# A planned one-core kernel on Trainium2: one weight step moved from ScalarE to VectorE, row-group products placed whole, column sums placed first

## The chip, the cores and the metric

The kernel runs on one core of a Trainium2 chip. The metric is the device time of one execution in microseconds (us). The engines are TensorE (PE; its weight loads PEld), VectorE (DVE), ScalarE (ACT), GpSimd (POOL) and SyncE (SP), which here only issues DMAs. The profiler gives the granted TensorE clock of each stretch, 1.00 for the upper of its two levels (2.4 GHz) and 0.50 for the lower (1.2 GHz).

## The reference

Three layers on 3072 tokens (4 sequences of 768), with a width of 256. The weight matrices are float64 and arrive as two 32-bit words a number; the kernel turns them into float32 itself.

```python
# 1: gated linear attention, 8 heads of 32, state of 16; cum = running sum of log a
y  = (C B^T * exp(cum_i - cum_j) * causal) x  +  C state * exp(cum)
state = exp(sum(log a)) * state + sum_j (B_j x_j) * exp(cum_last - cum_j)
# 2: gated feed-forward, d_ff = 1536
xn = y / sqrt(mean(y*y) + 1e-6) * rms_g
x  = (silu(xn @ w_gate) * (xn @ w_val)) @ w_out
# 3: channel mix, d_ff = 1024; x_prev is x one token earlier
xk, xr = mu_k*x + (1-mu_k)*x_prev, mu_r*x + (1-mu_r)*x_prev
out = sigmoid(xr @ w_r) * (relu(xk @ w_k)**2 @ w_v)
```

## The kernel before

**Tiles.** The tokens go in 6 tiles of 512 (128 of each sequence). Tile c has an attention stage (scores, masks, state products y), a norm, a first feed-forward stage `ffn1` of 12 units and a second one `ffn2` of 8 units. While `ffn1` of tile t runs, the attention of tile t + 1 is placed between its units (`attend`). For t = 0 there is no `ffn2` yet; `ffn2` of tile t - 1 follows `ffn1` of tile t. Each large product is made of three matmuls of 128 x 128 by 512 columns (`mm3`, L613 to L617): weight high part by input high part (L615), low by high (L616), high by low (L617).

**PSUM.** There are eight banks: two (`pacc`) accumulate `ffn1`'s output and serve the scores of tile 0, four (`pmm`) hold the gate and value products of two units and the first exponents, two (`patt`, tag `at`) are used in turn for the exponents, the scores and the state products of the later tiles.

**Start.** `sums_e` (L328) takes the logarithm of the decays, scans it on VectorE and sums it over columns with four small products `cumt` (L338); VectorE writes `cum` (L339). `spread_e` (L341) builds exponents in PSUM with a mask product (L346) and a product on `sums` (L347), and `exp_e` (L349) makes E of them on ScalarE, with `cum` as bias (recorded at L116, like all activations with a table). The exponentials of tiles 0 and 1 are made so; for the later tiles E is loaded and scanned. `chains` holds pairs of instructions that the planner must keep in order; the tables of ScalarE (exponential and logarithm, silu, sigmoid) are ordered in this way, so the first silu comes behind the last exponential of tile 1.

**Scores.** `scores` (L427) multiplies B and C. For tiles 0 and 1 (`plain`) it uses rows 0 to 31 for one bank and rows 32 to 63 for the other (L441); for tile 2 (`parity`) 16 rows at 0 and at 32 (L448); the later tiles use all rows (L454). `mask` (L473) multiplies a bank by E on VectorE, half by half. `y_two` (L509) begins with state products on rows 0 to 63 and 64 to 127 into two banks (L515), then adds the products with x (L486) and the state's update (L492).

**Weights.** 31 pieces of 512 KB are loaded by SyncE (L236) into two staging tiles and converted two at a time by `convert` (L243): `magnitude` makes a scaled float32 of the upper word on ScalarE (L255) and the top three bits of the lower word on ScalarE (L256); `move` clamps on VectorE (L260); `merge` puts sign, exponent and bits together in two VectorE instructions (L265, L267); `parts` rounds to the high part on ScalarE (L276) and subtracts for the low part on VectorE (L277). The loads of a later pair wait for L267.

**Order.** The program is first written in a natural order; then `arrange` (L1111) fixes the order on each engine. `Order` (L928) plays the instructions through with a price for each (`price`, L985) and always takes the ready one that comes first in the program. A PSUM or SBUF tile with several buffers can be begun only in its turn and when a buffer is free (`can`, L1032). An instruction needs only the tiles that it touches itself, so the products of a score group that write the first bank can be placed while the second is still in use. On the chip each engine follows the fixed order.

Of the kernel before, what the change touches and what calls it, by code (L numbers as in the profile page):

```python
# [16 lines left out]
P = 128  # L17
# [50 lines left out]
def tile_kernel(ctx: ExitStack, tc, a_c, x_t, B_t, B_s, C_s, B_p, C_p, C_h, kc,  # L68
                w_gate, w_val, w_out, w_k, w_v, w_r, out):
    nc = tc.nc  # L70
    slots, chains = {}, []

    class Pool:
        def __init__(self, name, bufs, space=None):
# [168 lines left out]
    def convert(j):  # L243
        js = range(j, min(j + 2, len(wjobs)))
        st = staged.pop(j // 2).rearrange("p i a b -> p (i a b)").rearrange("p (n w) -> p n w", w=2)
        t2w = t4("wt2", I32, "Cs" if j % 4 else "wt")
        tw = t2w.rearrange("p i n -> p (i n)")

        def part(i):
            s = slice(0, T * len(js)) if i is None else slice(T * i, T * i + T)  # L250
            return st[:, s, 0], st[:, s, 1], tw[:, s]

        def magnitude(i=None):
            lo, hi, t = part(i)
            nc.scalar.activation(out=t.bitcast(F32), in_=hi.bitcast(F32), func=AF.Copy, scale=2.0 ** -112)  # L255
            nc.scalar.activation(out=lo, in_=lo.bitcast(U32), func=AF.Copy, scale=TOP3[0], bias=TOP3[1])  # L256

        def move(i=None):
            lo, hi, t = part(i)
            nc.vector.tensor_scalar(out=t.bitcast(F32), in0=t.bitcast(F32), scalar1=-W_MAX, scalar2=W_MAX,  # L260
                                    op0=ALU.max, op1=ALU.min)

        def merge(i=None):
            lo, hi, t = part(i)
            nc.vector.scalar_tensor_tensor(out=hi, in0=t, scalar=-0x80000000, in1=lo,  # L265
                                           op0=ALU.bitwise_and, op1=ALU.bitwise_or)
            nc.vector.scalar_tensor_tensor(out=t, in0=t, scalar=3, in1=hi,  # L267
                                           op0=ALU.logical_shift_left, op1=ALU.bitwise_or)

        def parts(i=None):  # L270
            for n, k in enumerate(js):
                if i not in (None, n):
                    continue
                _, wh, wl = wjobs[k]
                t = t2w[:, n, :].rearrange("p (k m) -> p k m", k=2).bitcast(F32)
                nc.scalar.copy(wh, t)  # L276
                (vec_e if k in SUB_DVE else pool_e).tensor_tensor(out=wl, in0=t, in1=f32(wh), op=ALU.subtract)  # L277

        return magnitude, move, merge, parts
# [48 lines left out]
    def sums_e(a_sb):  # L328
        nc.vector.memset(f32(sums), 0.0)
        ln = t2("ln")[:RE]  # L330
        tabled(out=ln, in_=a_sb[:RE], func=AF.Ln)
        nc.vector.tensor_tensor_scan(out=ln, data0=starts.rearrange("p h i -> p (h i)"), data1=ln, initial=0.0,
                                     op0=ALU.mult, op1=ALU.add)
        nc.vector.tensor_copy(sums[:RE], ln)
        nc.vector.tensor_tensor(out=sums[32:32 + RE], in0=ln, in1=f32(sums[:RE]), op=ALU.subtract)
        ps = patt.tile([P, T], F32, tag="at", name="cumt")[:, :4 * RE].rearrange("p (h r) -> p h r", h=4)
        for h in range(4):
            nc.tensor.matmul(ps[:, h], sums[:, h * P:(h + 1) * P], pick, start=True, stop=True)  # L338
        nc.vector.tensor_scalar(out=cum, in0=ps, scalar1=-1.0, scalar2=None, op0=ALU.mult)  # L339

    def spread_e(c, b):  # L341
        for half in range(2):
# [20 lines left out]
    def parity(c):  # L363
        return c == 2
# [62 lines left out]
    def scores(c, b):  # L427
# [8 lines left out]
        if plain(c):  # L436
            br, cr = d.pop(("Br", b)), d.pop(("Cr", b))
            for q in range(2):
                for half in range(2):
                    g = slice(32 * half, 32 * half + 32)  # L440
                    nc.tensor.matmul(bank[half][:, q * 256:(q + 1) * 256], br[g, q, :],  # L441
                                     cr[g, 2 * q:2 * q + 2, :].rearrange("p a i -> p (a i)"), start=True, stop=True)
        elif parity(c):
            br, cr = d.pop(("Br", b)), d.pop(("Cr", b))
            for p in range(4):
                for j in range(2):
                    g = slice(32 * j, 32 * j + N)
                    nc.tensor.matmul(bank[j][:, p * P:(p + 1) * P], br[g, p, :], cr[g, p, :], start=True, stop=True)  # L448
        else:
            bs, cs = d.pop(("Bs", b)), d.pop(("Cs", b))  # L450
            for half in range(2):
                for q in range(2):
                    p = 2 * half + q
                    nc.tensor.matmul(bank[half][:, q * 256:(q + 1) * 256], bs[:, p, :],  # L454
                                     cs[:, p, :, :].rearrange("p a i -> p (a i)"), start=True, stop=True)
# [53 lines left out]
    def y_two(c, b):  # L509
        d = A[c]  # L510
        y = [patt.tile([P, T], F32, tag="at", name="y") for _ in range(2)]
        for k in range(2):
            for half in range(2):
                g = slice(64 * half, 64 * half + 64)
                nc.tensor.matmul(y[half][:, k * P:(k + 1) * P], Sf[g, b + k].rearrange("p h d -> p (h d)"),  # L515
                                 d["Ch"][g, b + k, :], start=k == 0, stop=False, skip_group_check=True)
        for k in range(2):
            y_x(y, (k * P, k * P), c, b + k, False)
            if c + 1 < NC:
                d["up", b + k] = y[k][:, 2 * P:2 * P + 2 * D]  # L520
                y_st(d["up", b + k], c, b + k)
# [230 lines left out]
        w_load()  # L752
    first, second = steps(), steps()
    clip(a_sb)
    sums_e(a_sb)
    spread_e(0, 0)
    scores(0, 0)
    spread_e(0, 1)
    for b in range(NB):
        for half in range(2):  # L760
# [145 lines left out]
        held[t] = x2  # L906
    mix(NC - 1, held.pop(NC - 1), act_e, vec_e)
    ffn2(NC - 1, lambda *_: None)
    arrange(tc, list(nc.cur_bb.bb.instructions), slots, chains)

# [15 lines left out]
class Order:  # L928
    SIGNAL, LANDING, RATE = 90.0, 1900.0, 270.0

    def __init__(self, instructions, slots, chains):
        self.slots, self.ins = slots, []
        where = {}
        for i in instructions:
            kind = type(i).__name__
# [9 lines left out]
        writes, reads = {}, {}  # L945
        for k, i in enumerate(self.ins):
            rs, ws = ([self.region(a, slots) for a in s if hasattr(a, "bass_ap")] for s in (i.ins, i.outs))
            for name, r in rs + ws:
                if name in slots and name not in self.tiles[k]:
                    self.tiles[k].append(name)  # L950
                    self.touch.setdefault(name, []).append(k)
# [33 lines left out]
    def price(self, i):  # L985
# [9 lines left out]
                return 20 + 1.7 * n * part, 200.0, False  # L995
            return (228.5 if n >= T else max(n / 2.4 + 15, 45.0)), 180.0, False
        if e == ACT_:
            return (1280.0, 0.0, False) if kind == "InstLoadActFuncSet" else (75 + 0.88 * n, 70.0, False)
        two = kind == "InstTensorTensor" or getattr(i, "is_scalar_tensor_tensor", False)
        if e == POOL_:  # L1000
            return (100 + 2.3 * n, 50.0, True) if kind == "InstTensorTensor" else (100 + 0.5 * n, 50.0, False)
# [7 lines left out]
    def run(self):  # L1009
# [20 lines left out]
        t, serial, order, held, holder = 0.0, 0, [], set(), None  # L1030

        def can(k):  # L1032
            return all(m in held or m in first.get(k, ()) and rank[m] == turn[self.slots[m][1]]
                       and free[self.slots[m][1]] > 0 for m in self.tiles[k])

        def release(j):
            left[j] -= 1
# [70 lines left out]
        return t, order  # L1108


def arrange(tc, instructions, slots, chains):  # L1111
    o = Order(instructions, slots, chains)
    _, order = o.run()
    last = {}
    for k in order:
# [43 lines left out]
```

## Time and profile before

| | |
|---|---|
| median of 3 runs | 542.84 us (542.33 to 543.45) |
| the profiled execution | 542.75 us, of it the span 541.0 us |
| granted TensorE clock, mean | 0.986 |
| TensorE busy | 530.0 us (98%) |
| VectorE busy | 403.1 us (75%) |
| ScalarE busy | 315.0 us (58%) |
| GpSimd busy | 14.4 us (3%) |
| matmuls | 2831 |
| HBM read, written | 38.38 MB, 3.34 MB |

The busy shares are averages over a start, in which the attention of tile 0, the weights and the norm are made, and a long steady stretch. TensorE's busy time also counts matmuls at the lower clock and short matmuls in full, so the stretches are read beside the granted clock.

### The profile page before, as it was taken

The page shows a single profiled execution, that of the slowest core. Times are in us where ns is not written, and L with a number is a line of the kernel's source. Part 1 is how long each engine was busy: PE and PEld are TensorE (multiplying, and loading weights), DVE is VectorE, ACT ScalarE, POOL GpSimd, SP SyncE. Part 2 cuts the span into 40 slices and gives each one's busy share as a digit, 9 for nine tenths or more (in the row PEclk, how much of TensorE's full clock was granted, in tenths as well). Part 3 has the DMA queues.
Part 4 walks back from the last instruction along what each step waited for, and adds up shares of the span by engine and source line. Part 5 has one row for each costly group of instructions (what it writes and reads, how often), then busy time and mean ns, then how long its engine had stood idle before and what let it go on. Part 6 is the DMA issues. An engine that isn't in the chain of part 4 may idle for free.

```text
span 541.0 us, 7496 instructions
## 1 busy us (share of the span) xinstructions
PE 530.0 (98%) x2831; PEld 421.4 (78%) x2831; DVE 403.1 (75%) x640; ACT 315.0 (58%) x546; POOL 14.4 (3%) x30
## 2 busy tenths in 40 slices
PE   8979999999999999999999999999999999999997
PEld 5646777787778888888888888888887888888885
DVE  5797889999999986596986597986454873335672
ACT  3998557954745864355774356774337662345562
POOL 4000000000002000001000001000000000000000
PEclk9987999999989999999999999999999999999999
DMA  8552456533426011316011315011000010000001
GB/s 261 157 179 93 170 166 220 199 89 113 131 59 184 32 41 39 117 43 184 29 39 40 117 44 171 1 40 39 1 0 2 1 39 1 0 0 1 18 22 39
DMA packets 21635, 42.20 MB, mean 78 GB/s; under 512 B 2064, under 2 KB 4880, under 8 KB 21600
## 3 DMA queue, kind: packets, MB, share of 16 engines
q1 hardware_dynamic: 19296, 33.34, 18.9%
q10 hardware_dynamic: 2304, 8.39, 4.8%
q8 instruction: 22, 0.36, 0.3%
q14 instruction: 13, 0.11, 0.1%
HBM read 38.38 MB, written 3.34 MB: 77 GB/s over the span
## 4 chain that ended last, share of the span: by engine, by line
PE 71%; DVE 2%; issue 0%; DVEq 0%
PE v L617 8%; PE v L616 8%; PE v L615 8%; PE x L616 5%; PE x L617 5%; PE x L615 5%; PE g L615 4%; PE g L617 4%; PE g L616 4%; PE kp L615 4%; PE kp L617 4%; PE kp L616 4%; PE y L486 1%; PE sc L454 1%; PE rps L617 1%; PE rps L616 1%
## 5 line engine op out<-in xcount | busy, mean ns | idle before, releaser
L646 DVE TENSOR_TENSOR hf<-sl,v 128x512 f32<-128x512 f32 x72 | 49.2, 684 | 53.9 <-PE v L617 49.8
L128 ACT CAST h<-hf 128x512 fp32r<-128x512 f32 x72 | 44.5, 619 | 69.3 <-DVE hf L646 64.8
L116 ACT ACTIVATE sl<-g 128x512 f32<-128x512 f32 x72 | 42.7, 594 | 48.3 <-PE g L617 48.3
L131 DVE TENSOR_TENSOR h<-hf,h 128x512 fp32r<-128x512 f32 x72 | 50.5, 703 | 23.7 <-ACT h L128 23.4
L615 PE MATMUL g<-xn,wgh 128*128 128x512 f32 x144 | 58.5, 408 | 0.3 <-ACT sl L116 0.3
L617 PE MATMUL v<-xn,wvh 128*128 128x512 f32 x144 | 57.8, 401 | 0.0
L616 PE MATMUL v<-xn,wvl 128*128 128x512 f32 x144 | 57.8, 401 | 0.0
L617 PE MATMUL g<-xn,wgh 128*128 128x512 f32 x144 | 57.2, 397 | 0.0
L616 PE MATMUL g<-xn,wgl 128*128 128x512 f32 x144 | 57.1, 397 | 0.0
L615 PE MATMUL v<-xn,wvh 128*128 128x512 f32 x144 | 57.1, 400 | 0.0
L615 PE MATMUL x<-h,woh 128*128 128x512 f32 x144 | 56.9, 395 | 0.0
L616 PE MATMUL x<-h,wol 128*128 128x512 f32 x144 | 56.9, 395 | 0.0
L617 PE MATMUL x<-h,woh 128*128 128x512 f32 x144 | 56.0, 393 | 0.0
L712 DVE TENSOR_TENSOR k<-rl 128x512 f32<-128x512 f32 x48 | 34.6, 724 | 15.3 <-ACT rl L711 15.0
L128 ACT CAST h<-k 128x512 fp32r<-128x512 f32 x48 | 29.6, 619 | 16.7 <-DVE k L712 16.5
L131 DVE TENSOR_TENSOR h<-k,h 128x512 fp32r<-128x512 f32 x48 | 32.6, 685 | 7.2 <-ACT h L128 6.7
L711 ACT ACTIVATE rl<-kp 128x512 f32<-128x512 f32 x48 | 28.6, 595 | 15.9 <-PE kp L617 15.3
L617 PE MATMUL v<-h,wvvh 128*128 128x512 f32 x96 | 37.8, 394 | 0.0
L617 PE MATMUL kp<-xm,wkh 128*128 128x512 f32 x96 | 37.8, 393 | 0.0
L615 PE MATMUL kp<-xm,wkh 128*128 128x512 f32 x96 | 37.7, 393 | 0.0
L616 PE MATMUL v<-h,wvvl 128*128 128x512 f32 x96 | 37.6, 392 | 0.0
L616 PE MATMUL kp<-xm,wkl 128*128 128x512 f32 x96 | 37.6, 392 | 0.0
(135 smaller groups left out, 1058.1 us busy)
## 6 DMA issues: line engine op xcount, KB each, us to landing
E<-la_r ACTq DMA_DIRECT2D x16, 512.0 KB
x<-in_x_t SPq DMA_DIRECT2D x6, 512.0 KB
wst<-in_w_gate SPq DMA_DIRECT2D x6, 512.0 KB
wst<-in_w_val SPq DMA_DIRECT2D x6, 512.0 KB
wst<-in_w_out SPq DMA_DIRECT2D x6, 512.0 KB
Br<-in_B_s SPq DMA_DIRECT2D x12, 256.0 KB
Cr<-in_C_s SPq DMA_DIRECT2D x12, 256.0 KB
out<-r SPq DMA_DIRECT2D x12, 256.0 KB
```

Source lines behind the costliest of these rows:

```text
L116: ins.append(lambda: nc.scalar.activation(out=out, in_=in_, func=func, **kw))
L128: nc.scalar.copy(x[:, 0, :], src)
L131: last[0] = le.tensor_tensor(out=x[:, 1, :], in0=src, in1=f32(x[:, 0, :]), op=ALU.subtract).ins
L454: nc.tensor.matmul(bank[half][:, q * 256:(q + 1) * 256], bs[:, p, :], cs[:, p, :, :].rearrange("p a i -> p (a i)"), start=True, stop=True)
L486: nc.tensor.matmul(y[half][32 * j:32 * j + 32, at[half]:at[half] + P], x[:, b, h * D:(h + 1) * D], m[:, h, :], start=start and at[half] == ...
L615: nc.tensor.matmul(ps, w[0][:, k, ws], x[:, 0, :], start=first, stop=False)
L616: nc.tensor.matmul(ps, w[1][:, k, ws], x[:, 0, :], start=False, stop=False)
L617: nc.tensor.matmul(ps, w[0][:, k, ws], x[:, 1, :], start=False, stop=last)
L646: nc.vector.tensor_mul(hf, sl, v)
L711: nc.scalar.activation(out=rl, in_=kp, func=AF.Relu)
L712: nc.vector.tensor_mul(k2, rl, rl)
```

## The change

Four things are changed, three of them in the planner. (1) For the first four weight pieces (j < 4, the first two calls of `convert`) the top three bits of the lower word come from a shift on VectorE in place of the activation L256. (2) The first product of each score group of the tiles 0 to 2 and the first state product of `y_two` are noted with the names of both banks; the planner places them only when both can be begun (`can` now counts several buffers of one tag). (3) The first product of the first scores is chained behind the last of the column sums. (4) The planner's price of a ScalarE operation is 60 + 0.94 n ns above 128 columns and 250 ns up to there, with 100 ns to its result, in place of 75 + 0.88 n and 70 ns. All other instructions are the same; their order is planned anew.

```diff
         def magnitude(i=None):
             lo, hi, t = part(i)
+            if j < 4:
+                nc.scalar.activation(out=t.bitcast(F32), in_=hi.bitcast(F32), func=AF.Copy, scale=2.0 ** -112)
+                nc.vector.tensor_scalar(out=lo, in0=lo, scalar1=29, scalar2=None, op0=ALU.logical_shift_right)
+                return
             nc.scalar.activation(out=t.bitcast(F32), in_=hi.bitcast(F32), func=AF.Copy, scale=2.0 ** -112)
             nc.scalar.activation(out=lo, in_=lo.bitcast(U32), func=AF.Copy, scale=TOP3[0], bias=TOP3[1])
...
-            nc.tensor.matmul(ps[:, h], sums[:, h * P:(h + 1) * P], pick, start=True, stop=True)
+            mm = nc.tensor.matmul(ps[:, h], sums[:, h * P:(h + 1) * P], pick, start=True, stop=True)
         nc.vector.tensor_scalar(out=cum, in0=ps, scalar1=-1.0, scalar2=None, op0=ALU.mult)
+        return mm.ins.name
...
+                    if q + half == 0:
+                        groups.append((mm.ins.name, [t.name for t in bank]))
...
+                    if p + j == 0:
+                        groups.append((mm.ins.name, [t.name for t in bank]))
...
+                if k + half == 0:
+                    groups.append((mm.ins.name, [t.name for t in y]))
...
-    sums_e(a_sb)
+    cumt = sums_e(a_sb)
     spread_e(0, 0)
     scores(0, 0)
+    chains.append((cumt, groups[0][0]))
...
-            for name, r in rs + ws:
+            for name in [name for name, _ in rs + ws] + groups.get(i.name, []):
                 if name in slots and name not in self.tiles[k]:
...
-            return (1280.0, 0.0, False) if kind == "InstLoadActFuncSet" else (75 + 0.88 * n, 70.0, False)
+            return (1280.0, 0.0, False) if kind == "InstLoadActFuncSet" else ((60 + 0.94 * n if n > P else 250.0), 100.0, False)
...
         def can(k):
-            return all(m in held or m in first.get(k, ()) and rank[m] == turn[self.slots[m][1]]
-                       and free[self.slots[m][1]] > 0 for m in self.tiles[k])
+            new = {}
+            for m in sorted((m for m in self.tiles[k] if m not in held), key=rank.get):
+                tag = self.slots[m][1]
+                j = new[tag] = new.get(tag, -1) + 1
+                if m not in first.get(k, ()) or rank[m] != turn[tag] + j or free[tag] <= j:
+                    return False
+            return True
```

## Rows read from the trace of the kernel before

**Rows 1.** Busy time by stretch; columns PE, PEld, DVE, ACT, POOL, clock, DMA share, GB/s.

```profile
10.44:17.00 6.56, 5.59 (x46) 3.44 (x45) 2.80 (x5) 6.56 (x26) 1.00 (x3) 1.00 0.89 314
17.00:33.00 16.00, 12.66 (x117) 8.10 (x114) 14.20 (x29) 15.61 (x40) 0.65 (x2) 0.93 0.52 157
33.00:44.30 11.30, 10.23 (x40) 6.56 (x39) 9.69 (x18) 11.28 (x30) 0.00 (x0) 0.95 0.53 184
44.30:51.20 6.90, 6.90 (x16) 4.58 (x15) 5.62 (x8) 5.66 (x9) 0.00 (x0) 0.51 0.16 52
51.20:85.00 33.80, 33.80 (x183) 24.95 (x182) 29.19 (x43) 20.69 (x32) 0.00 (x0) 1.00 0.49 161
85.00:107.00 22.00, 21.97 (x143) 16.83 (x142) 21.41 (x32) 19.06 (x28) 0.10 (x1) 1.00 0.64 216
107.00:165.00 58.00, 57.41 (x367) 45.47 (x366) 57.41 (x85) 31.01 (x53) 0.00 (x0) 0.97 0.32 95
...
200.00:536.40 336.40, 336.40 (x1744) 275.77 (x1743) 223.00 (x357) 178.52 (x294) 4.35 (x4) 1.00 0.12 40
```

**Rows 2.** Time order of the start: start us, us, engine, line, operation, count.

```profile
8.05 1.13 PE L441 MATMUL sc<-Cr,Br 32*128 32x256 f32 x8
9.37 0.69 PE L338 MATMUL cumt<-pick,sums 128*128 128x16 f32 x4
9.57 0.47 SPq L384 DMA_DIRECT2D Cr<-in_C_p  x1
10.44 6.31 ACT L116 ACTIVATE E<-Eb,cum 128x128 f32<-128x128 f32 x24 [5.58 <-PE Eb L347]
```

**Rows 3.** Time order of ScalarE ahead of the first silu.

```profile
21.27 1.20 ACT L256 ACTIVATE wst<-wst 128x1024 int32<-128x1024 uint32 x1
22.33 1.20 ACT L255 ACTIVATE wt<-wst 128x1024 f32<-128x1024 f32 x1
23.41 0.66 ACT L505 COPY yT<-y 128x256 f32<-128x256 f32 x2
...
43.04 1.28 ACT L115 ACT_TABLE_LOAD   x1
```

**Rows 4.** VectorE by line and form, 0:170: count, busy us, mean ns, idle before.

```profile
L265 DVE SCALAR_TENSOR_TENSOR wst<-wt,wst 128x1024 int32<-128x1024 int32 x13 | 15.9, 1224 | 0.8 <-ACT wst L256 0.4
...
L260 DVE TENSOR_SCALAR wt<-wt 128x1024 f32<-128x1024 f32 x13 | 8.9, 688 | 0.2 <-ACT wt L255 0.2
```

**Rows 5.** Time order of TensorE: score groups (L441, L448) and state products (L515).

```profile
19.20 1.13 PE L441 MATMUL sc<-Cr,Br 32*128 32x256 f32 x8
...
62.99 1.12 PE L441 MATMUL sc<-Cr,Br 32*128 32x256 f32 x4
...
70.33 0.69 PE L441 MATMUL sc<-Cr,Br 32*128 32x256 f32 x2
...
78.51 0.71 PE L515 MATMUL y<-Ch,Sf 64*128 64x128 f32 x4
...
86.51 1.12 PE L441 MATMUL sc<-Cr,Br 32*128 32x256 f32 x6
...
92.35 0.72 PE L515 MATMUL y<-Ch,Sf 64*128 64x128 f32 x8
...
122.30 1.16 PE L448 MATMUL sc<-Cr,Br 16*128 16x128 f32 x16
...
151.07 2.41 PE L448 MATMUL sc<-Cr,Br 16*128 16x128 f32 x16 [0.16 <-DVE E L473]
```

**Rows 6.** Time order: last masks of tile 1, its normed input's cast and first use.

```profile
88.14 0.68 DVE L473 TENSOR_TENSOR E<-sc,E 128x512 f32<-128x512 f32 x1
...
89.80 0.69 DVE L473 TENSOR_TENSOR E<-sc,E 128x512 f32<-128x512 f32 x1
...
106.03 0.62 ACT L128 CAST xn<-xnf 128x512 fp32r<-128x512 f32 x1
...
106.71 0.39 PE L615 MATMUL g<-xn,wgh 128*128 128x512 f32 x1
```

More of the change, by code (lines that the diff above doesn't have):

```diff
@@ L70, in tile_kernel @@
     nc = tc.nc
-    slots, chains = {}, []
+    slots, chains, groups = {}, [], []
     class Pool:
@@ L440, in scores @@
                     g = slice(32 * half, 32 * half + 32)
-                    nc.tensor.matmul(bank[half][:, q * 256:(q + 1) * 256], br[g, q, :],
+                    mm = nc.tensor.matmul(bank[half][:, q * 256:(q + 1) * 256], br[g, q, :],
                                      cr[g, 2 * q:2 * q + 2, :].rearrange("p a i -> p (a i)"), start=True, stop=True)
+                    if q + half == 0:
+                        groups.append((mm.ins.name, [t.name for t in bank]))
         elif parity(c):
@@ L447, in scores @@
                     g = slice(32 * j, 32 * j + N)
-                    nc.tensor.matmul(bank[j][:, p * P:(p + 1) * P], br[g, p, :], cr[g, p, :], start=True, stop=True)
+                    mm = nc.tensor.matmul(bank[j][:, p * P:(p + 1) * P], br[g, p, :], cr[g, p, :], start=True, stop=True)
+                    if p + j == 0:
+                        groups.append((mm.ins.name, [t.name for t in bank]))
         else:
@@ L514, in y_two @@
                 g = slice(64 * half, 64 * half + 64)
-                nc.tensor.matmul(y[half][:, k * P:(k + 1) * P], Sf[g, b + k].rearrange("p h d -> p (h d)"),
+                mm = nc.tensor.matmul(y[half][:, k * P:(k + 1) * P], Sf[g, b + k].rearrange("p h d -> p (h d)"),
                                  d["Ch"][g, b + k, :], start=k == 0, stop=False, skip_group_check=True)
+                if k + half == 0:
+                    groups.append((mm.ins.name, [t.name for t in y]))
         for k in range(2):
@@ L908, in tile_kernel @@
     ffn2(NC - 1, lambda *_: None)
-    arrange(tc, list(nc.cur_bb.bb.instructions), slots, chains)
+    arrange(tc, list(nc.cur_bb.bb.instructions), slots, chains, groups)
 ENGINES = (mybir.EngineType.PE, mybir.EngineType.DVE, mybir.EngineType.Activation, mybir.EngineType.Pool,
@@ L929, with __init__ @@
     SIGNAL, LANDING, RATE = 90.0, 1900.0, 270.0
-    def __init__(self, instructions, slots, chains):
+    def __init__(self, instructions, slots, chains, groups):
         self.slots, self.ins = slots, []
+        groups = dict(groups)
         where = {}
@@ L1108, in run, with arrange @@
         return t, order
-def arrange(tc, instructions, slots, chains):
-    o = Order(instructions, slots, chains)
+def arrange(tc, instructions, slots, chains, groups):
+    o = Order(instructions, slots, chains, groups)
     _, order = o.run()
```

## The prediction

> **What bounds the kernel now.** I read the busy time by stretch first. From 44.3 us to 536.4 us TensorE hardly runs out of work (its largest loss in a stretch is 0.6 us, in 107:165), and from 200 us on it is busy 336.40 of 336.40 us at the full clock [rows 1]. So from the first gating product on, the end is set by how soon that stream starts and by how much TensorE work it holds; the last matmul to the end of the span (4.6 us) does not change. Ahead of 44.3 us the limit is another engine: ScalarE is busy 6.56 of 6.56, 15.61 of 16.00 and 11.28 of 11.30 us, while TensorE and VectorE have gaps [rows 1]. The time order of that stretch tells what ScalarE must get through: 24 exponentials of tile 0 that start at 10.44 us and wait for a product of TensorE, the first weight pieces, the norm, the exponentials of tile 1, and then a table load at 43.04 us that lets the first silu run [rows 2, 3]. Four PSUM banks hold the gate and value products, so until that silu TensorE can do little of the stream.
>
> A second limit stands behind. VectorE has 1.28 + 4.61 + 0.59 + 0.59 = 7.07 us idle between 44.3 and 165 us, and of that only 1.18 us lie behind 85 us [rows 1]. Whatever TensorE saves there is worth something only as far as VectorE keeps up. Third, the granted clock: 0.51 in the stretch 44.3:51.2 (the lower level, 1.2 GHz, nearly throughout) and 0.97 in 107:165, about 1.00 elsewhere behind 44 us [rows 1]. That is (1 - 0.51) x 6.9 = 3.4 us and (1 - 0.97) x 58 = 1.7 us of full-clock work not done. Ahead of the first, TensorE worked through short products between waits (10.23 of 11.30 us busy in 33:44.3); within the second stretch a score group took 2.41 us [rows 1, 5].
>
> **Column sums ahead of the first scores.** Now the first score group runs at 8.05 us for 1.13 us, the column sums only at 9.37 us, and the exponentials start at 10.44 us [rows 2]. With the chain, the sums and then the products that the exponentials wait for come first. TensorE may fill the wait with the second pair of mask products, so the gain lies between nothing and 1.13 us; I take 0.9. The scores move behind by as much; they are needed only when four exponentials, about 4 x 0.263 us (6.31 / 24), are done [rows 2], so that is hidden; if it were not, the first mask would be late by at most 1.13 us. SyncE's reload of the scores' operand buffer, issued at 9.57 us, waits for these scores and comes later by the same, with the loads queued behind it; it is for tile 1, whose scores behind 51 us start at 62.99 us, so it is hidden too [rows 2, 5].
>
> **Top bits on VectorE.** Two ScalarE activations of 1024 columns go. The first holds ScalarE for 22.33 - 21.27 = 1.06 us [rows 3], the second is of the same form: 2.1 us in all. The first sits right where the last exponentials of tile 0 have ended and the copy of y waits (23.41 us), on the way to the norm [rows 3]; the second belongs to the next pair and stands ahead of the first weight cast, while the norm's sum is still being made. As ScalarE is busy nearly throughout, both count, but the second may partly leave a hole in which ScalarE waits for TensorE: I take 1.6 us of 2.1 (bounds 0 and 2.1). Two one-source shifts on VectorE come in, in place, on every second word. No row has that form. The nearest are the one-source clamp, 688 ns for 1024 columns, and the two-source merge that reads the same strided words, 1224 ns [rows 4]. I take 0.69 us, the row with one source; 1.4 us in all, bounds 1.4 and 2.4. Their cover: VectorE is idle 16.00 - 14.20 = 1.8 us in 17:33 and 1.6 us in 33:44.3 [rows 1]. They wait only for the landed weights, no longer for ScalarE, and the merge behind them loses its wait for ScalarE. At 1.4 us they fit; at 2.4 us 0.6 us would spill into the norm chain that VectorE works through before the first gate product. The weight DMAs of the next pieces are issued when the second merge is done, so they move with it and with nothing else.
>
> The page "VectorE: DVE Perf Modes" of the Trainium skill (What auto-detection actually checks) says that a one-source operation from SBUF to SBUF with an even count handles two elements at a time, and names no condition on the stride for 4-byte elements; the clamp's row agrees for unit stride, and no run here shows stride two. By that rule the price is the lower bound, and the sum is the one I use.
>
> **Row groups wait for all banks.** A score group writes two banks from two groups of rows. Whole, it takes 1.13 us (x8); a half (x4) or six of eight take 1.13 or 1.12 us too, and a quarter (x2) 0.69 us [rows 5]. So a split group pays twice. In tile 1's scores behind 51 us the six pieces (from 62.99 to 86.51 us: x4, x4, x2, x2, x2, x6) take 1.12 + 1.13 + 3 x 0.69 + 1.12 = 5.4 us for 2.5 groups, worth 2.8 us whole: 2.6 us go. The state products of the same stage run as 0.71 + 0.71 us against 0.72 us whole [rows 5]: 0.7 us. Together 3.3 us in the stretch 51.2:107. In tile 2 one group takes 2.41 us against 1.16 us [rows 5]: 1.25 us in 107:165, the largest loss there. The scores of the later tiles use full rows and are not touched.
>
> The wait itself: the group's first product is not placed before both banks are free. Nothing is queued behind it, since the planner takes the next ready instruction; TensorE has gating products to go on with. What waits is the pair of masks on VectorE and then the state products. The banks of one pair come free one mask apart, for instance 88.14 and 89.80 us, 1.66 us [rows 6].
>
> How much of this arrives at the end? In 51.2:85 VectorE idles 4.6 us, waiting for TensorE, so the 3.3 us fit. In 107:165 it is busy 57.41 of 58 us: I credit nothing of the 1.25 us there, bounds 0 and 1.25. For the clock I also credit nothing, bounds 0 and 3.4 + 1.7.
>
> **The planner's new prices.** ScalarE's small operations rise from 188 to 250 ns (measured: 263), 512 columns from 526 to 541 ns. This reorders all engines a little. No row shows its cost. From the nearest rows I bound it by one stretch at the low clock, 1.7 us, on either side, and take nothing.
>
> **Sum.** 0.9 + 1.6 + 3.3 = 5.8 us. The profiled execution took 542.75 us (span 541.0), within 0.1 us of the median 542.84, so 542.75 - 5.8 = 537.0 us.
>
> **Rivals.** *The clock comes along (0.20).* If the start is denser and groups are whole, the low stretch behind 44 us may vanish; VectorE's 7.07 us of room would hold 3.3 + 3.4. Then 537.0 - 3.4 = 533.6; with the second low stretch too, 531.9. For it speaks that both low stretches follow broken TensorE work; against it that TensorE still waits for the exponentials, as now.
>
> *VectorE takes it back (0.24).* VectorE is as full as TensorE from 85 us on, and gets 1.4 to 2.4 us more. If the convert steps in 44:85 are not done sooner, TensorE meets weights that aren't ready, the 3.3 us become waits, and of the start's 2.5 us the shifts eat up to 1.2: 540.2 to 541.5, about 541.
>
> *The held scores make the next tile late (0.16, slower).* Tile 1's normed input must be there when the first tile's units end. Its second cast starts at 106.03 us and the first product on it at 106.71 us [rows 6]: no slack shows. Three of the four score groups ran in pieces and would now start one bank later (the last already went as six of eight): 3 x 1.66 = 5.0 us at most. The chain from there to the input would come 5.0 us later, less the start's 2.5 us: 2.5 us late, and TensorE's savings turn into a gap ahead of tile 1: 542.75 + 2.5 = 545.2. It decides once the delays add up to over 2.5 us. Against it: the chain's own VectorE steps queue behind converts in a stretch where VectorE is busy 21.41 of 22.00 us [rows 1], so it isn't a chain without slack, and part of the delay would be taken up there.
>
> The page "TensorEngine Tiling (Array Packing)" of the Trainium skill (Gotcha 1: PSUM Pressure) says that row tiles write different banks, which raises the pressure on PSUM; the two banks a group takes here agree with it, and it speaks for this rival.
>
> *The change doesn't do what it says*: if the shift runs at the two-source price, or groups still come apart behind their first product, the time is that of the VectorE rival, whose chance holds this.
>
> **How the numbers follow.** Forecast 0.40, clock 0.20, VectorE 0.24, late tile 0.16. Predicted: 537.0, its own range 535 to 539.5. Leaving out the slow rival (0.16) and the extreme of the clock rival, the range is 531.5 to 543.0: the upper end takes in the VectorE rival with the planner's 1.7 us. About 0.2%, 1.1 us, is what a measurement of this kernel can tell from no change. Faster: 0.40 + 0.20 + 0.11 of the VectorE rival = 0.71; same 0.13; slower 0.16.
>
> **What would show it.** Sums: the first exponential at about 9.5 us in place of 10.44. Shift: two VectorE rows of 0.69 us near 17 to 25 us, and the table load ahead of the first silu near 40.5 us in place of 43.04. Groups: scores and state products of tiles 1 and 2 only as x8 or x16, about 1.13 us each, and the first product of tile 1 that reads its normed input near 101 us in place of 106.71. VectorE rival: TensorE waits for VectorE between 50 and 165 us. Late tile: a TensorE gap at the end of the first tile. The forecast is wrong if the silu starts no sooner than 43 us, or if TensorE idles over 2 us in 51:165.

## The result, and the profile after

| | before | after |
|---|---|---|
| median (runs) | 542.59 us (538.71 to 543.45, 4) | 535.83 us (535.27 to 536.12, 4) |
| profiled execution, its span | 542.75, 541.0 | 535.56, 533.1 |
| mean granted clock of that execution | 0.986 | 0.993 |
| first exponential starts | 10.44 | 9.36 |
| table load ahead of the first silu | 43.04 | 42.43 |
| first product on tile 1's normed input | 106.71 | 101.27 |
| first product of the first mix (`kp`) | 168.17 | 160.37 |

The ratio of the times is 0.9888, 95% interval 0.9839 to 0.9936: by the interval 3.5 to 8.7 us faster, by the medians 6.8 us. Executions of one and the same kernel differ with their mean granted clock (last section), so where a difference is small I also compare runs of like clock. Ratios leave out runs that took over 1.5% longer than the fastest of the same kernel; only one kernel below, the one with the new prices alone, had such runs.

From `kp` on nothing changed: 541.0 - 168.17 = 372.8 us to the end of the span before, 533.1 - 160.37 = 372.7 us after. So all of it was won ahead of `kp`. The busy time by stretch of the kernel after, columns as in [rows 1]:

```profile
17.00:33.00 16.00, 11.37 (x102) 7.28 (x92) 14.83 (x31) 13.39 (x33) 0.41 (x1) 0.93 0.53 157
33.00:44.30 11.30, 9.64 (x39) 6.34 (x37) 11.15 (x18) 11.27 (x33) 0.00 (x0) 0.94 0.53 187
44.30:51.20 6.90, 6.83 (x23) 5.49 (x24) 6.83 (x10) 6.86 (x11) 0.00 (x0) 0.75 0.24 67
51.20:85.00 33.80, 33.74 (x202) 25.82 (x201) 31.74 (x46) 22.54 (x35) 0.00 (x0) 1.00 0.58 200
85.00:107.00 22.00, 21.47 (x141) 16.35 (x139) 21.83 (x33) 18.61 (x28) 0.11 (x1) 1.00 0.44 145
107.00:165.00 58.00, 55.43 (x378) 44.40 (x378) 57.42 (x87) 32.85 (x54) 3.51 (x2) 1.00 0.41 129
...
200.00:528.50 328.50, 328.50 (x1708) 269.17 (x1707) 215.65 (x346) 173.24 (x285) 4.13 (x4) 1.00 0.12 40
```

Against [rows 1]: the clock behind 44 us rose from 0.51 to 0.75 and in 107:165 from 0.97 to 1.00. VectorE fills 11.15 of 11.30 and 6.83 of 6.90 us where it filled 9.69 and 5.62. TensorE now idles 2.57 us in 107:165, before 0.59. The same view over everything ahead of `kp`, the kernel before and then the kernel after:

```profile
0.00:168.17 168.17, 161.09 (x947) 119.29 (x948) 149.26 (x235) 114.24 (x217) 6.97 (x25) 0.96 0.48 155
```

```profile
0.00:160.37 160.37, 149.76 (x948) 112.30 (x949) 149.23 (x236) 112.86 (x215) 7.13 (x25) 0.98 0.50 163
```

TensorE's busy time fell by 161.09 - 149.76 = 11.3 us, more than the end moved, and its idle time rose from 7.08 to 10.61 us. VectorE's busy time stayed (149.26 and 149.23 us), and its idle time fell from 18.91 to 11.14 us. Busy and idle time of any engine add up to the time of `kp`, so these sums say where time went and not yet which engine set it. The part behind 44.3 us tells more, before and after:

```profile
44.30:168.17 123.87, 123.24 (x718) 94.42 (x717) 116.73 (x174) 78.87 (x123) 0.21 (x2) 0.96 0.43 137
```

```profile
44.30:160.37 116.07, 112.83 (x717) 88.24 (x718) 113.31 (x169) 78.65 (x122) 0.21 (x2) 0.99 0.44 146
```

Before, TensorE idles 0.6 us there and VectorE 7.1 us: TensorE was the limit. After, they idle 3.2 and 2.8 us, and neither has much room. The 7.8 us are 4.4 us less idle time of VectorE and 3.4 us of its work that was done ahead of 44.3 us. What VectorE waited for longest between 44.3 us and `kp` (columns: total us, times, longest us), before:

```profile
DVE hf L646 <- PE v L617: 5.5, 3, 2.0
```

and after:

```profile
DVE hf L657 <- PE v L628: 1.3, 1, 1.3
```

VectorE's idle time by place (sums over the stretches above and the start): ahead of 44.3 us it fell by 3.4 us, of which the two shifts fill 1.4; in 44.3:85 by 3.8 us, behind 85 us by 0.6 us.

The start, in the time order of ScalarE after the change, answers [rows 2, 3]:

```profile
9.36 5.00 ACT L116 ACTIVATE E<-Eb,cum 128x128 f32<-128x128 f32 x19 [4.50 <-PE Eb L352]
...
42.43 1.28 ACT L115 ACT_TABLE_LOAD   x1
43.72 0.60 ACT L116 ACTIVATE sl<-g 128x512 f32<-128x512 f32 x1
```

The exponentials start 1.08 us sooner, the silu only 0.6 us. In 17:33 ScalarE is busy 13.39 us where it was busy 15.61: what the two activations freed became waiting. Three of its waits ahead of 45 us, of which only the first had a row before (5.6 us):

```profile
ACT E L116 <- PE Eb L352: 4.5, 1, 4.5
ACT rs L116 <- PE ss L581: 1.3, 1, 1.3
ACT yT L514 <- PE y L501: 0.7, 1, 0.7
```

The shifts in VectorE's time order, an operation that [rows 4] could only bound:

```profile
15.46 0.68 DVE L257 TENSOR_SCALAR wst<-wst 128x1024 int32<-128x1024 int32 x1
...
20.17 0.69 DVE L257 TENSOR_SCALAR wst<-wst 128x1024 int32<-128x1024 int32 x1
```

And the groups in TensorE's time order, to be read against [rows 5]; every group of tiles 1 and 2 is placed whole now, twelve of them in all (tile 1's first, at 41.87 us, still takes 1.73 us, since TensorE waits in its middle for ScalarE's exponentials):

```profile
57.83 1.13 PE L446 MATMUL sc<-Cr,Br 32*128 32x256 f32 x8
64.60 1.13 PE L446 MATMUL sc<-Cr,Br 32*128 32x256 f32 x8
73.76 0.72 PE L524 MATMUL y<-Ch,Sf 64*128 64x128 f32 x8
80.94 1.13 PE L446 MATMUL sc<-Cr,Br 32*128 32x256 f32 x8
...
133.14 1.16 PE L455 MATMUL sc<-Cr,Br 16*128 16x128 f32 x16
```

### The profile page after: what moved, and what is told of

Same layout as the page of the kernel before. It is cut to its first block, busy times and chain, and to the rows that moved or that the text cites. A ratio compares the mean times of both kernels' runs of the same rounds, so it can differ in the third digit from the quotient of the medians.

```text
span 533.1 us, 7496 instructions
## 1 busy us (share of the span) xinstructions
PE 518.7 (97%) x2831; PEld 414.4 (78%) x2831; DVE 403.0 (76%) x642; ACT 313.3 (59%) x544; POOL 14.7 (3%) x30
## 4 chain that ended last, share of the span: by engine, by line
PE 72%; DVE 2%; issue 0%; ACT 0%; DVEq 0%
PE v L628 9%; PE v L627 8%; PE v L626 8%; PE x L628 5%; PE x L627 5%; PE x L626 5%; PE g L626 4%; PE g L628 4%; PE g L627 4%; PE kp L626 4%; PE kp L628 4%; PE kp L627 4%; PE y L495 1%; PE sc L463 1%; PE rps L628 1%; PE rps L627 1%
## 5 line engine op out<-in xcount | busy, mean ns | idle before, releaser
L628 PE MATMUL v<-xn,wvh 128*128 128x512 f32 x144 | 56.7, 394 | 0.0
L626 PE MATMUL v<-xn,wvh 128*128 128x512 f32 x144 | 56.5, 396 | 0.2 <-ACT sl L116 0.2
```

The costliest lines, as they stand in the source:

```text
L626: nc.tensor.matmul(ps, w[0][:, k, ws], x[:, 0, :], start=first, stop=False)
L628: nc.tensor.matmul(ps, w[0][:, k, ws], x[:, 1, :], start=False, stop=last)
```

## Experiments

My theory after the result: whole groups are what pays, the freed ScalarE time and the earlier sums add less, and VectorE limits what TensorE can give. Rivals: the new order that the planner made by its prices, and the granted clock. As the planner lays out all engines anew after any edit, the groups and the shift were also tried inside a fixed plan, in which only the one thing moves; the chain was tried only so, the prices only planned again. All comparisons are with the kernel before on the same chip (medians 542.6 to 542.9 us there).

**The changed kernel again.** No edit.

> The changed kernel itself, to stand beside the others with as many runs. 535 to 537 us expected; if its fast runs spread as widely as those of before (538.7 to 544.8), the clock's luck is in it too, if they spread by 1 us it isn't.

535.99 us (535.30 to 537.84), ratio 0.9888 [0.9844, 0.9931]. The gain stands. Its profiled execution took 537.84 us, with the clock at 0.56 in 29.75:36 and 0.72 in 140:150 where the other one had 0.73 and 1.00.

**Only whole groups, in the plan of before.** After planning, all products of a row group go to the place of the group's last product on TensorE. The other engines keep their order.

```diff
     _, order = o.run()
+    order = gather(o, order, whole)   # at[product] = place of its group's last product
```

> The plan of before, unchanged but for one thing: the products of each score group of tiles 0 to 2 and of each pair of state products are gathered at the place of the group's last one; VectorE, ScalarE and the DMA queues keep their order. If whole groups are what the change brings, TensorE saves 3.3 us in 51:107 and 1.2 us or more behind it, and the low clock behind 151 us goes (1.7 us): 537 to 539 us against 542.8. If the gain comes from the start or from the planner's new order, this stays within 1.5 us of before. If VectorE takes TensorE's savings back, 541 to 542 with TensorE waits between 85 and 165 us.

539.24 us (538.68 to 540.01), ratio 0.9958 [0.9932, 0.9984]. Behind 44.3 us:

```profile
44.30:164.53 120.23, 116.81 (x719) 90.42 (x719) 117.59 (x176) 78.42 (x122) 0.21 (x2) 0.97 0.44 142
```

Of the changed kernel's 7.8 us at `kp`, 168.17 - 164.53 = 3.6 us come in this execution from moving some dozens of short products. VectorE's idle time is down to 2.6 us, as in the changed kernel, but it has 117.59 us of work left where that one has 113.31. So whole groups take away VectorE's waits for TensorE, and the rest of the gain is work that VectorE had done sooner. Not all groups are whole: tile 1's first, one of its pairs of state products and two of tile 2's groups still come in pieces, most of them since TensorE keeps to its order and waits in their middle. The end of one of them:

```profile
148.34 1.15 PE L452 MATMUL sc<-Cr,Br 16*128 16x128 f32 x14 [0.72 <-DVE E L480]
```

**Groups taken apart, in the plan of after.** The second half of each of five score groups goes six stream products later on TensorE.

```diff
     _, order = o.run()
+    order = part_groups(o, order, whole)   # second bank's products: six 512-column products later
```

> The plan of the changed kernel, but of five score groups (the last three of tile 1, the last two of tile 2) the second half's products stand six stream products later on TensorE; all other engines keep their order. If a split group costs TensorE its second 1.1 us and TensorE is the limit: 5 x 1.1 = 5.7 us more, 541 to 542, and a further 1.7 us for each low stretch of the clock that comes back. If VectorE is the limit there: 1 to 3 us more. If splitting is harmless: within 1 us of the changed kernel.

543.13 us (538.28 to 544.53), ratio 1.0007 [0.9974, 1.0039]: 7.1 us slower than the changed kernel beside it, its whole gain. In the time order of TensorE each half takes as long as the whole did:

```profile
57.76 1.12 PE L446 MATMUL sc<-Cr,Br 32*128 32x256 f32 x4
60.41 1.13 PE L446 MATMUL sc<-Cr,Br 32*128 32x256 f32 x4
```

```profile
44.30:168.25 123.95, 121.87 (x717) 94.11 (x718) 114.38 (x171) 78.64 (x121) 0.21 (x2) 0.96 0.42 134
```

Five groups at 1.1 us explain 5.6 of TensorE's 121.87 - 112.83 = 9.0 us more busy time; the clock behind 44.3 us is also lower, 0.96 in place of 0.99. VectorE idles 9.6 us there again, TensorE 2.1 us. That the clock falls with the groups isn't shown: one of the ten runs had 0.996 and took 538.28 us, and the one at 0.989 took 540.78 us, 4.9 us more than the changed kernel's median of 535.9 us at 0.989 and 0.990.

**Only the wait for all banks, planned again.** The wait without the shift, the chain and the prices.

```diff
-            for name, r in rs + ws:
+            for name in [name for name, _ in rs + ws] + groups.get(i.name, []):
```

> Only the wait for all banks is put into the planner of before, old prices, no shift, no chain; all engines are planned anew. If whole groups carry the gain: 537 to 540. If their wait makes the attention of tile 1 late: 543 to 545.

544.28 us (541.42 to 546.50), ratio 1.0042 [1.0010, 1.0075]: slower. The time order of TensorE shows two score groups of tile 1 still in pieces:

```profile
54.85 0.69 PE L442 MATMUL sc<-Cr,Br 32*128 32x256 f32 x2
56.13 0.69 PE L442 MATMUL sc<-Cr,Br 32*128 32x256 f32 x2
57.42 0.70 PE L442 MATMUL sc<-Cr,Br 32*128 32x256 f32 x4
66.27 0.70 PE L442 MATMUL sc<-Cr,Br 32*128 32x256 f32 x4
68.03 0.69 PE L442 MATMUL sc<-Cr,Br 32*128 32x256 f32 x2
69.79 0.69 PE L442 MATMUL sc<-Cr,Br 32*128 32x256 f32 x2
```

The wait holds back a group's first product until both banks are free; nothing holds the rest behind it, and here the planner put gating products in between. The wait is not the same thing as whole groups. Why the kernel is slower than before is open: TensorE's busy time ahead of `kp` fell to 155.43 us, but its idle time rose to 169.84 - 155.43 = 14.4 us.

**All but the wait, planned again.**

```diff
-    arrange(tc, list(nc.cur_bb.bb.instructions), slots, chains, groups)
+    arrange(tc, list(nc.cur_bb.bb.instructions), slots, chains, [])
```

> The changed kernel with the groups' wait taken out of the planner, all planned anew: shift, chain and prices alone. If whole groups carry the gain: 540 to 543. If the start and the prices do: 536 to 538.

546.56 us (541.60 to 547.10), ratio 1.0058 [1.0015, 1.0101]: shift, chain and prices without the wait are slower than the kernel before. Five of its seven runs had a mean clock of 0.983; the other two, at 0.989 and 0.994, took 541.73 and 541.60 us. The profiled one ran at 0.61 in 20:29.75 and had its first gating product at 37.81 us (before: 32.93), so a part of its loss lies in the start and not in the groups.

**Only the shift, in the plan of before.** The two instructions change engines at their place.

```diff
+            if j < 4:
+                ...
+                nc.vector.tensor_scalar(out=lo, in0=lo, scalar1=29, scalar2=None, op0=ALU.logical_shift_right)
```

> The plan of before, with the two top-bits steps run on VectorE, each at its planned place in time; nothing else moves. If ScalarE's 2.1 us ahead of the first silu count, the silu comes 1 to 2 us sooner and the time is 541 to 542. If ScalarE only waits elsewhere (for TensorE's exponent products), the silu and the time stay within 0.5 us of before. The shift itself: 0.69 us by the one-source clamp, 1.22 us by the merge.

542.40 us (539.41 to 543.75), ratio 1.0013 [0.9984, 1.0043]: nothing. Its profiled execution ran at 0.68 in 20:29.75, so its trace can't be used for the size.

**The shift undone, in the plan of after.** The top bits go back to ScalarE, at their place.

```diff
-                nc.vector.tensor_scalar(out=lo, in0=lo, scalar1=29, scalar2=None, op0=ALU.logical_shift_right)
+                nc.scalar.activation(out=lo, in_=lo.bitcast(U32), func=AF.Copy, scale=TOP3[0], bias=TOP3[1])
```

> The plan of the changed kernel, but the top bits of the first four pieces are made on ScalarE again, each where the plan has the shift in time; nothing else moves. If ScalarE's relief carries part of the gain: 1 to 2 us more, with the silu 1 to 2 us later. If it is only shuffled: within 0.5 us.

538.28 us (537.31 to 539.61), ratio 0.9928 [0.9907, 0.9949]: 2.3 us slower than the changed kernel. In the time order of ScalarE the table load comes 2.5 us later than in the changed kernel (42.43), and `kp` at 162.38 in place of 160.37:

```profile
44.92 1.28 ACT L115 ACT_TABLE_LOAD   x1
```

So in the plan of after the shift is worth what two activations cost, while in the plan of before it was worth nothing that could be measured. Both plans were laid out for the engine on which they had the step.

**The chain undone, in the plan of after.** The first scores' products stand ahead of the column sums on TensorE again.

```diff
     _, order = o.run()
+    order = ahead(o, order, whole)   # first scores right ahead of the column sums
```

> The changed kernel with one thing undone in TensorE's order: the four products of the first scores stand ahead of the column sums again; every other instruction of every engine keeps its place. Theory (the chain is a real but small part of the start): the first exponential goes back from 9.36 to near 10.4 us and the time from 536.0 to about 536.9, at most 537.1. Rival (ScalarE's start is not the end of any chain, what it begins earlier it only waits for later): the exponential moves by 1 us all the same and the time stays within 0.3 us of 536.0.

536.86 us (535.19 to 538.57), ratio 0.9888 [0.9856, 0.9920]. The ratio is that of the changed kernel, and the runs overlap; the times don't tell 0.9 us from nothing. The trace does: against the repeat of the changed kernel, whose low stretches lie alike, the first exponential is at 9.80 in place of 8.95 us, the table load at 43.21 in place of 42.61, and `kp` at 163.40 in place of 162.74. 0.85 us at the start arrive as about 0.7 us, as far as one pair of executions tells: the first exponential of the changed kernel itself came once at 9.36 and once at 8.95 us.

**Only the new prices, planned again.** The kernel before with the new price line.

```diff
-            return (1280.0, 0.0, False) if kind == "InstLoadActFuncSet" else (75 + 0.88 * n, 70.0, False)
+            return (1280.0, 0.0, False) if kind == "InstLoadActFuncSet" else ((60 + 0.94 * n if n > P else 250.0), 100.0, False)
```

> Only ScalarE's new prices in the planner, nothing else. If the plan's order is what counts, 538 to 541; if the prices only shuffle, within 1.7 us of before on either side.

541.71 us (538.74 to 548.38), ratio 1.0006 [0.9962, 1.0050]: not told from before. Four of the ten runs had a mean clock of 0.975 and took 547.74 to 548.38 us; the other six have a median of 541.0 us, and two of these at 0.994 took 538.74 and 539.75 us, as the kernel before does at that clock (539.24).

**The changed kernel with the old prices, planned again.** The line above turned round.

> The changed kernel with the old price of ScalarE's instructions in the planner, and so with another order of the work, but with the shift, the wait for all banks and the chain. Theory (the new prices do nothing of their own): 535 to 537 us. Rival (the parts need the order that these prices make, as the parts that were planned again alone suggest): 538.5 to 544 us, with split or late groups, or waits of TensorE over 2 us that the changed kernel does not have.

540.72 us (539.99 to 542.81), ratio 0.9974 [0.9953, 0.9996]: 4.7 us slower than the changed kernel. The waits of TensorE and its time order show two things that differ:

```profile
PE g L626 <- ACT xn L128: 6.8, 1, 6.8
```

```profile
81.42 0.69 PE L446 MATMUL sc<-Cr,Br 32*128 32x256 f32 x2
86.39 1.13 PE L446 MATMUL sc<-Cr,Br 32*128 32x256 f32 x6
...
104.66 0.48 PE L455 MATMUL sc<-Cr,Br 16*128 16x128 f32 x2
112.61 1.15 PE L455 MATMUL sc<-Cr,Br 16*128 16x128 f32 x14
```

The first gating product comes at 33.76 us (31.11 in the changed kernel), behind a wait for the normed input; and with the wait for all banks in force three score groups (two shown) come apart. So the prices do little alone and much in company: with them the plan starts sooner and places every group whole. No run had a third set of prices, so whether these prices matter or any small shake of the planner does as much isn't shown.

**The silu ahead of the last weight cast, in the plan of after.** In the changed kernel TensorE waits at 145 us, here in its time order and then in ScalarE's:

```profile
145.30 0.50 PE L626 MATMUL g<-xn,wgh 128*128 128x512 f32 x1 [2.38 <-ACT sl L116]
147.15 0.50 PE L626 MATMUL v<-xn,wvh 128*128 128x512 f32 x1 [0.20 <-ACT sl L116]
```

```profile
142.58 0.62 ACT L280 CAST wvvh<-wt 128x512 fp32r<-128x512 f32 x1 [2.61 <-DVE wt L271]
143.10 1.65 ACT L128 CAST xm<-xf 128x512 fp32r<-128x512 f32 x3
144.66 0.58 ACT L116 ACTIVATE sl<-g 128x512 f32<-128x512 f32 x1
```

The silu has its input but stands behind a cast that waits for VectorE. If that order is the cause, moving the silu frees 2.4 us.

```diff
     _, order = o.run()
+    order = ahead(o, order, whole)   # at[first silu behind the last weight cast] = at[cast] - 0.5
```

> The changed kernel with one thing moved on ScalarE: the first silu that stands behind the cast of the last weight piece goes ahead of that cast; TensorE, VectorE and the DMA queue keep their order. In the changed kernel that cast waits 2.6 us for VectorE at 142 us, the silu stands behind it, and TensorE waits 2.4 us for the silu at 145 us. Theory (the time forecast beyond 536 is given back in this in-order wait): TensorE's wait at 145 us is below 0.5 us, last tile ends 2 to 2.5 us earlier, time 533.3 to 534.2. Rival (VectorE itself is the limit of 140:150, the silu is only where it shows): a wait of 2 us or more comes back within the next 6 us, behind VectorE, and the time is within 0.6 us of 536.0.

535.63 us (534.13 to 537.56), ratio 0.9871 [0.9840, 0.9903]: within 0.4 us of the changed kernel. The time orders of TensorE, ScalarE and VectorE in that kernel:

```profile
141.71 0.50 PE L628 MATMUL g<-xn,wgh 128*128 128x512 f32 x1
...
146.01 0.50 PE L628 MATMUL v<-xn,wvh 128*128 128x512 f32 x1 [2.64 <-ACT sl L116]
...
139.57 0.58 ACT L116 ACTIVATE sl<-g 128x512 f32<-128x512 f32 x1
...
145.32 0.68 DVE L660 TENSOR_TENSOR hf<-sl,v 128x512 f32<-128x512 f32 x1
```

The silu runs at 139.57, the gate product at 141.71 with no wait, and then the value product waits 2.64 us in its place, until 146.01: right behind VectorE's product `hf`, which ends at 145.32 + 0.68 = 146.00 and frees the bank. `hf` stands behind the last piece's convert, and VectorE is busy 9.97 of the 10 us in 140:150. The profile names the silu for that wait, but the one that ends last is VectorE. So the rival holds: the wait belongs to VectorE, and ScalarE's order only chose which product takes it.

**Twelve more products in TensorE's gap, in the plan of after.** The warm-up on a constant tile gets twelve more products, placed in the idle stretch ahead of 29.75 us.

```diff
-    warm_up(WARM[1], pacc, "acc")
+    warm_up(WARM[1] + 12, pacc, "acc")   # the twelve stand ahead of the exponentials' next product
```

> The changed kernel with twelve more products on a constant tile (some 2.7 us of TensorE by the rows of the warm-up products) in the idle stretch of TensorE from 26.0 to 29.75 us; nothing else moves. The changed kernel has one interval of low granted clock of 3.4 us near 31 us, right behind that idle stretch, and another near 45 us. Theory (low intervals follow an idle stretch that lies right ahead of them): the interval near 31 us is gone or later, and tile 1's products get up to 1.7 us back where TensorE is the limit; since ScalarE is the limit from 33 to 44 us, the time is 535.0 to 536.0. Rival (the extra products delay ScalarE's start of tile 1): 536.3 to 538.

536.53 us (533.43 to 537.62), ratio 0.9888 [0.9856, 0.9921]. The busy time by stretch of its profiled execution, and of the changed kernel's:

```profile
26.00:29.75 3.75, 2.78 (x13) 1.93 (x11) 3.53 (x11) 3.72 (x13) 0.00 (x0) 1.00 0.80 270
29.75:36.00 6.25, 4.54 (x19) 3.04 (x18) 6.21 (x12) 6.04 (x15) 0.00 (x0) 1.00 0.30 78
```

```profile
26.00:29.75 3.75, 0.03 (x1) 0.00 (x0) 3.57 (x10) 3.72 (x12) 0.00 (x0) 1.00 0.80 275
29.75:36.00 6.25, 5.50 (x17) 3.79 (x17) 6.16 (x13) 5.83 (x14) 0.00 (x0) 0.73 0.27 62
```

With the gap filled this execution has no low stretch at all (mean clock 1.00), `kp` at 158.32 us and 533.43 us in all, the fastest seen. But three of its six runs had a mean clock of 0.985 or 0.986 and took 537.6 us. Filling this gap doesn't keep the clock up in each run; where the low stretches of those three lay is not on record, and what decides it stays open.

No version beats the changed kernel by more than the runs scatter.

## Why the prediction was right, point by point

**Total.** Forecast 537.0, own range 535 to 539.5; measured 535.83. The likeliest case came in the time, but not all of its mechanism, so the close match is in part luck. Whole groups paid as forecast. Both signs that the prediction had named for a wrong forecast came too: the silu started at 43.72 us, not ahead of 43, and TensorE idled 0.06 + 0.53 + 2.57 = 3.2 us in 51.2:165. And the parts, tested one at a time, don't add up to the whole.

**At like clock the sum is close.** The 69 runs of the kernel before beside the experiments cluster: 34 at a mean clock of 0.987 with a median of 543.14 us, 11 at 0.994 with 539.24 us. On a straight line between these, 0.990 stands for 543.14 - 3/7 x 3.90 = 541.5 us. Six of the eight runs of the changed kernel have 0.989 or 0.990, with a median of 535.9 us. So by this estimate 5.6 us are left at like clock, against the 5.8 of the sum; the other 1.2 us of the 6.8 would be the clock, which I had credited with nothing (bounds 0 and 5.1), about a quarter of the rival *the clock comes along*. The estimate is rough: no run of the kernel before had 0.988 to 0.990, and its one run at 0.991 took 543.22 us.

**Column sums.** Forecast 0.9. The size agrees: 0.85 us at the first exponential, about 0.7 at `kp` when undone. Expected near 9.5 us, seen at 9.36. One pair of executions shows it, and the start scatters: with the order of before the first exponential came at 10.44, 10.47 and 9.93 us (the kernel before, whole groups alone, the shift alone).

**Top bits.** The price of a shift was the row I took, 0.69 us. The page "VectorE: DVE Perf Modes" of the Trainium skill (What auto-detection actually checks) lets a one-source operation within SBUF on an even count handle two elements at a time and sets no condition on the stride for that. The trace agrees: 0.68 and 0.69 us on every second word against 0.688 us for the clamp on neighbouring words [rows 4]. The gain of 1.6 us was a little low in the plan of after (2.0 at `kp`, 2.3 in the medians, about the full 2.1) and is nothing that could be measured in the plan of before. The sign I named for it failed: the table load should have come near 40.5 us and came at 42.43. I had read the start's gain off a single engine. Ahead of the table load ScalarE does the same operations as before less the two activations; what they freed came back as 2.4 us of waits between the first exponential and the table load, above all 1.3 us for the norm's sum and 0.7 us for a product, where before none is listed. The plan of after without the shift has its table load at 44.92 us, 1.9 us later than before in spite of the earlier exponentials. So within that plan the shift does bring the silu sooner, as forecast; what failed is that the new plan, which I had taken as the old one less its terms, has its silu later. How the shift then reaches `kp` shows behind 44.3 us, here without it:

```profile
44.30:162.38 118.08, 114.32 (x725) 89.16 (x725) 115.85 (x176) 81.19 (x126) 0.21 (x2) 0.99 0.45 142
```

VectorE idles 2.2 us there, no more than the 2.8 us of the changed kernel, but it has 115.85 - 113.31 = 2.5 us more work left, and `kp` comes 2.0 us later. By the words of the prediction, a silu no sooner than 43 us meant that the forecast is wrong; it came at 43.72 and the time held, so that test was badly chosen: VectorE's work and idle time behind the start were the better sign.

**Whole groups.** Right in kind: all groups placed whole, 1.13 and 1.16 us each but for tile 1's first, tile 1's normed input used at 101.27 (forecast near 101). In size the 3.3 us stand between 2.8 us (groups alone in the plan of before, nine of whose ten runs have 0.989; by the straight line 543.14 - 2/7 x 3.90 = 542.0 against 539.2) and more in the plan of after, where taking five groups apart costs 7.1 us in the medians and 4.9 us at like clock. The weight loads of the 2.41 us group [rows 5] show that it was two halves in turn, the second behind VectorE's mask, which the one row of x16 hides:

```profile
151.07 0.96 PEld L448 LDWEIGHTS sc<-Cr,Br 16*128 16x128 f32 x8 [0.59 <-DVE E L473]
152.32 0.96 PEld L448 LDWEIGHTS sc<-Cr,Br 16*128 16x128 f32 x8 [0.30 <-DVE E L473]
```

The prediction missed another one: tile 2's third group came as two halves of 1.15 us, at 138.04 and 139.54 us. What failed is the step that took the wait for the cause of whole groups: planned alone it left tile 1's scores in pieces, and the time went up by 0.4%.

**The planner's prices.** This is the term that was mis-sized: nothing, bounds 1.7 us either way. Alone that holds (541.0 us by the six runs at 0.987 to 0.994, 1.6 us under the 542.6 beside it). Within the change they are worth 4.7 us (540.72 against 535.99), outside my bounds. The total fits in part because I priced the groups as whole, and in this plan they are whole only with these prices.

**VectorE.** The rival that takes the gain back (541) was wrong in its time and right in its place. TensorE idles 2.57 us in 107:165, over the 2 us that I had named as a sign of a wrong forecast, and the run with the moved silu shows that VectorE holds it there. TensorE's busy time in 107:165 fell by 57.41 - 55.43 = 2.0 us, and all of it turned into idle time; the sum had left tile 2's groups and the clock there at nothing for this reason. It did not take the start's gain, since VectorE itself ran ahead: its holes up to 85 us shrank by 7.2 us.

**Held scores.** Did not happen. The four score groups of tile 1 were placed whole, three of them ran at one go, and the normed input came 5.4 us sooner. The Trainium skill ("TensorEngine Tiling (Array Packing)", Gotcha 1: PSUM Pressure) spoke for this rival; the two banks a group agree with it, but no tile came late by it here.

One figure ahead of the prediction is wrong: the weights come in 27 pieces, not 31. No term rests on it.

## What to carry to other kernels

Behind the start, set the idle time of each engine beside its work, up to the point behind which nothing changes. Here TensorE had 0.6 us idle and VectorE 7.1; once VectorE's were down to 2.8, what was taken off TensorE became waits, and what still moved `kp` was VectorE's work done sooner. Products of two row groups that run side by side cost the whole again for each half that is placed apart, so look for rows with less than the full count; and see that the planner keeps them together, since a wait ahead of the first product alone does not. A row that counts a whole group can hide a wait in its middle; the rows of the weight loads show it. Where a planner lays out all engines anew, parts of a change don't add up: test each part inside a fixed plan, and take the planner's own prices for a part of the change.

## What the runs showed of the hardware

- The same program draws different clocks from run to run: mean 0.979 to 1.00 in the 69 runs of the kernel before, mostly 0.987 (543.14 us) or 0.994 (539.24 us). 3.9 us between two clusters of one kernel are over half of what the change brought. The mean clock isn't all: the 34 runs at 0.987 themselves took 541.05 to 543.95 us.
- With the idle stretch of TensorE that lay ahead of a low one filled, one execution kept 1.00 throughout, and three of six had 0.985 or 0.986.
- Of a pair of row groups, one product into one bank takes 0.69 us, the two products of one bank 1.12 to 1.13 us, the whole 1.13 us, and four of its eight rows 0.70 us where, by this length, they are one product of each bank side by side (57.42 us, the wait planned alone); the halves of the state products take 0.71 and the whole 0.72 us.
- A shift on every second 32-bit word takes 0.69 us for 1024 columns on VectorE, as fast as a one-source operation on neighbouring words, while the two-source merge on the same words takes 1.22 us.
